# Linear attention and a softplus MLP on one core: the first tile's steps by a list, weights converted further ahead, q of the second tile on VectorE, the third batch's k maxima by GpSimd

## The chip, the cores and the metric

One core of one Trainium2 chip runs the kernel. The engines work side by side, each through its own queue in order: TensorE (PE, its weight loads PEld), VectorE (DVE), ScalarE (ACT), GpSimd (POOL) and SyncE (SP), whose queue starts nearly all transfers. The metric is device time in microseconds. Before the change three runs gave 912.88, 913.96 and 916.6 us, median 913.96.

## The reference

For each of 8 batches and 8 heads (576 tokens, 64 wide) q is turned into a softmax over its 64 channels and k into a softmax over its 576 tokens; `kv` is their sum over tokens, and the output of attention is the product of q's softmax with `kv`. All heads side by side give 4608 rows of 512 for the MLP.

```python
q_s = np.exp(q - np.max(q, axis=-1, keepdims=True))
q_s = q_s / (np.sum(q_s, axis=-1, keepdims=True) + 1e-09)
k_s = np.exp(k - np.max(k, axis=2, keepdims=True))
k_s = k_s / (np.sum(k_s, axis=2, keepdims=True) + 1e-09)
kv = np.einsum('bhsd,bhse->bhde', k_s, v)
x = np.einsum('bhsd,bhde->bhse', q_s, kv)       # then (4608, 512)
h = x @ w_in                                     # 512 to 2048
g = np.maximum(h, 0.0) + np.log1p(np.exp(-np.abs(h)))
out = g @ w_out                                  # 2048 to 512
```

## The kernel before

**Tiles and slots.** The 4608 rows are nine tiles of 512. A tile (t) has 16 slots (j), one for each 128 of the 2048 hidden columns: `up(t, j)` makes `ph` (128 hidden x 512 tokens) from x and a weight of w_in, `softplus` makes `l`, `split_g` parts it, and `down(t, j)` adds its product with w_out to the four accumulators `po`. All matmuls but the exact ones are done three times, with an operand in two parts: `hi` (rounded to the matmul's input type, ScalarE) and `lo` (the remainder, VectorE), as hi hi, lo hi, hi lo (L386 to L388 up, L418 to L420 down).

**Order.** The program is written slot by slot, and every engine takes its instructions in that order. In slot n stand `up(n)`, the slot's list of attention steps, then (before the change, tile 0 only) the weight steps, `split_g` of slot n-1, `softplus(n)`, in tile 0 the weight steps for three slots on, `down(n-2)`, and last the matmuls that the attention steps left in `waiting`. `ph` has two buffers.

**Weights.** A weight k is loaded once (L102, L103, both halves in tile `w{k}`) as 64-bit words, put together in tile 0 and kept. Per weight: `top_w` (L126) and `scale_w` (L121) on ScalarE; `sign_w`, in tile 0 on VectorE (L132), ahead of tile 0 for weights 0 to 2 on GpSimd (L134); `join_w` on VectorE (L142); and `split_w`, a cast on ScalarE (L151) and the remainder on VectorE (L152). `split_w(k)` writes into tile `w{k-1}` (weight 4 into `spare`), so it also waits until weight k-1 has been split. The first four slots of tile 0 are exact (`EXACT`): they use the joined weight itself (L381, L416) and are split only at the end of tile 0.

**Attention.** During tile t the attention of tile t+1 is made, by `PLAN`, a list of step names for each slot. `u{h}{i}` are the six steps of a k unit (a pair of heads h of one batch): 0 the maxima over a partition's tokens (L188), 1 `across` (L204), 2 subtract (L209), 3 exp and the products with v (L215, L220), 4 the reciprocal, 5 the parts of kv (L244, L247). Maxima across partitions come by two transposes on TensorE (L190, L205) while the batch number is at most `ON_PE`, and by a GpSimd reduction (L193) beyond it. `q{i}` are twelve steps of q's softmax over two halves: maxima 0, 1 (L284), 2 their swap (L271, L293), 3, 4 subtract (L296), 5, 6 exp (L299), 7, 8 totals (L302), 9 the reciprocals, 10, 11 multiply (L310); 3, 4, 10 and 11 of tile 1 go to GpSimd, of later tiles to VectorE. `x{h}{i}` transpose q (L327), take its parts (L331, L332) for the x products (L337 to L339), and part the result (L345, L346). Tile 0's own attention is made ahead of its slots from a written order; there `split_whole` (L255, L256) and `split_x0` (L373, L374) part kv and x of tile 0, in slots 0 and 1.

Of the kernel before, what the change touches and what calls it, by code (L numbers as in the profile page):

```python
# [23 lines left out]
HP = H // 2  # L24
NJ = DF // P
# [7 lines left out]

SUBS = [4] * 9

ON_PE = 2

EXACT = 4
START = [P * sum(SUBS[:t]) for t in range(len(SUBS) + 1)]
# [2 lines left out]
    "u00 u10", "u01 u11", "u02 u12", "u03 u13 q0", "u04 u14 u05 u15 q1 q2", "u20 u30 q3", "u21 u31 q4", "u22 u32",  # L42
    "u23 u33 q5 q6", "u24 u34 u25 u35 q7 q8 q9", "q10", "q11 x00 x01", "x02 x10 x11", "x12 x20 x21", "x30 x31", "",
    "x22 x32",
]
NTILE = len(SUBS)
TOK = P * max(SUBS)
# [15 lines left out]
def tile_attn_ffn(  # L63
# [9 lines left out]
    nc = tc.nc  # L73
# [65 lines left out]
    def join_w(k):  # L139

        low, high = words(k, U32)
        nc.vector.scalar_tensor_tensor(  # L142
            out=low, in0=high, scalar=3, in1=low, op0=ALU.logical_shift_left, op1=ALU.bitwise_or
        )
# [109 lines left out]
    def split_whole(h):  # L254
        nc.scalar.copy(kv_hi[0][h], whole[:, h])  # L255
        nc.vector.tensor_tensor(out=kv_lo[0][h], in0=whole[:, h], in1=kv_hi[0][h].bitcast(F32), op=ALU.subtract)  # L256
# [17 lines left out]
    def q_unit(t):  # L274

        n = TOK // 16
        half = [qtiles[t][:, 2 * g:2 * g + 2].rearrange("p h (i r) -> p (h i) r", r=32) for g in range(2)]
        m, s = (sm.tile([P, TOK // 8], F32, name=name) for name in ("m", "s"))

        def spread(a, g):  # L280
            return a[:, g * n:(g + 1) * n].unsqueeze(2).broadcast_to([P, n, 32])

        def top(g):
            nc.vector.tensor_reduce(out=m[:, g * n:(g + 1) * n], in_=half[g], op=ALU.max, axis=AX.X)  # L284

        copy = nc.vector.tensor_copy if t else nc.scalar.copy
        if t:
            slow = [nc.gpsimd if t == 1 else nc.vector] * 2
        else:
            slow = [nc.vector, nc.gpsimd]  # L290

        def join():
            nc.vector.tensor_tensor(out=m, in0=m, in1=swapped(m, copy), op=ALU.max)  # L293

        def shift(g):
            slow[g].tensor_tensor(out=half[g], in0=half[g], in1=spread(m, g), op=ALU.subtract)  # L296

        def power(g):
            nc.scalar.activation(half[g], half[g], AF.Exp)  # L299

        def total(g):
            nc.vector.tensor_reduce(out=s[:, g * n:(g + 1) * n], in_=half[g], op=ALU.add, axis=AX.X)  # L302

        def invert():
            o = swapped(s, copy)
            nc.vector.scalar_tensor_tensor(out=s, in0=s, scalar=EPS, in1=o, op0=ALU.add, op1=ALU.add)
            nc.vector.reciprocal(s, s)

        def divide(g):
            slow[g].tensor_tensor(out=half[g], in0=half[g], in1=spread(s, g), op=ALU.mult)  # L310

        return [
            lambda: top(0), lambda: top(1), join, lambda: shift(0), lambda: shift(1),
            lambda: power(0), lambda: power(1), lambda: total(0), lambda: total(1), invert, lambda: divide(0), lambda: divide(1),
        ]
# [55 lines left out]
    def split_x0(h):  # L371
        x = x_part(0, h)
        nc.scalar.copy(x[:, 0], x0[:, h])  # L373
        nc.vector.tensor_tensor(out=x[:, 1], in0=x0[:, h], in1=x[:, 0].bitcast(F32), op=ALU.subtract)  # L374
# [68 lines left out]
    with tc.manual_schedule():  # L443

        make_identity(nc, ident)
        q_load(0)
        for i in range(HP):
            place = dict(pool=xp, tag=f"x{i - 1}", shape=(P, HP * TOK)) if i >= 2 else {}
            kv_prefetch(engine=nc.vector, queue=nc.scalar, **place)
        for k in range(5):  # L450
            load_w(k)
        whole = wp.tile([P, HP, P], F32, name="spare")
        qT = wp.tile([P, HP, TOK], F32, name=f"w{NJ - 1}")
        x0 = xp.tile([P, HP, TOK], F32, name="x0")
        for z in [whole] + [z.bitcast(F32) for i in range(2) for z in kv_hi[i] + kv_lo[i]]:
            nc.vector.memset(z, 0.0)

        po = [ps_o.tile([P, DM], F32, name=f"po{h}") for h in range(HP)]  # L460
        units = [kv_unit(0, h, po[h]) for h in range(HP)]
        first = [x_first(h, po[h]) for h in range(HP)]
        todo = {f"q{i}": fn for i, fn in enumerate(q_unit(0))}
        for h in range(HP):
            todo.update({f"u{h}{i}": fn for i, fn in enumerate(units[h])})
            todo.update({f"x{h}{i}": fn for i, fn in enumerate(first[h])})
        for k in range(3):
            for name, fn in (("t", top_w), ("m", scale_w), ("s", lambda k: sign_w(k, nc.gpsimd)), ("j", join_w)):
                todo[f"{name}{k}"] = lambda k=k, fn=fn: fn(k)

        warm = ps_h.tile([P, TOK], F32, name="ph")
        todo["warm"] = lambda: [nc.tensor.matmul(warm[:, 0:P], lhsT=ident, rhs=ident, start=True, stop=True) for _ in range(8)]
        todo["kv"] = kv_prefetch
        todo["w"] = lambda: [load_w(k) for k in range(5, 10)]
        todo["q"] = lambda: [q_load(1)] + [load_w(k) for k in range(10, NJ)]
        for name in (
            "q0 q1 u00 q2 q3 q4 q5 u10 u01 u11 u02 u12 q6 u03 u13 u20 u30 u21 u31 u22 u32 t0 m0 s0 u23 u33 warm q7 q8 q9 "
            "kv kv w u04 u14 u05 u15 q10 q11 x00 x10 x01 x11 t1 m1 u24 u34 u25 u35 x20 x30 x21 x31 s1 j0 x02 x12 x22 x32 "
            "t2 m2 s2 j1 q"
        ).split():  # L480
            todo[name]()

        def attend(t):

            steps = [[] for _ in range(NJ + 1)]
            todo = {}

            def lazy(prefix, n, make):
                unit = []

                def step(i):
                    def fn():
                        if not unit:
                            unit.extend(make())
                        unit[i]()
                    return fn

                todo.update({f"{prefix}{i}": step(i) for i in range(n)})

            if t < B:  # L500
                for h in range(HP):
                    lazy(f"u{h}", 6, lambda h=h: kv_unit(t, h, banks[h % 2], after=kv_prefetch))
            lazy("q", 12, lambda: q_unit(t))
            for h in range(HP):
                lazy(f"x{h}", 3, lambda h=h: x_unit(t, h, banks[h % 2]))
            for s, names in enumerate(PLAN):
                steps[s] = [todo[name] for name in names.split() if name in todo]
            if t + 1 < NTILE:
                steps[14].append(lambda: q_load(t + 1))
            return steps  # L510

        order = [(t, j) for t in range(NTILE) for j in range(NJ)]
        pending, soft, waiting = [], None, []
        for n in range(len(order) + 3):
            slot = order[n] if n < len(order) else None
            if slot:
                t, j = slot
                if j == 0:
                    steps = attend(t + 1) if t + 1 < NTILE else [[] for _ in range(NJ + 1)]
                ph = up(t, j)  # L520
                for fn in steps[j]:
                    fn()
                if t == 0:
                    if j < 2:
                        split_whole(2 * j)
                        split_whole(2 * j + 1)
                    if j + 2 < NJ:
                        join_w(j + 2)
                        if j + 2 >= EXACT:
                            split_w(j + 2)  # L530
                    if j < 2:
                        split_x0(2 * j)
                        split_x0(2 * j + 1)
                if 0 <= n - (NJ - 2) < EXACT:
                    split_w(n - (NJ - 2))
                if j == NJ - 1:
                    for fn in steps[NJ]:
                        fn()
            if soft:
                pending.append((soft[0], soft[1] if exact(*soft[0]) else split_g(soft[1])))  # L540
                soft = None
            if slot:
                soft = slot, softplus(ph)
                if t == 0 and j + 3 < NJ:
                    for fn in (top_w, scale_w, sign_w):
                        fn(j + 3)
            while pending and order.index(pending[0][0]) <= n - 2:
                (t, j), g = pending.pop(0)
                down(t, j, g)
            for products in waiting:  # L550
                products()
            waiting.clear()
# [37 lines left out]
```

## Time and profile before

| | |
|---|---|
| profiled execution, its own time | 913.47 us |
| its span, first to last instruction | 911.7 us |
| granted TensorE clock, mean | 0.983 |
| TensorE busy | 867.4 us (95%) |
| VectorE busy | 413.3 us (45%) |
| ScalarE busy | 378.7 us (42%) |
| GpSimd busy | 50.5 us (6%) |
| DMA | 55.22 MB, 18.0% of 16 engines |

How to read it: the span is the time that the trace covers, and the rest of the execution lies around it. Busy times overlap between engines. A group of instructions is given with its line, engine, operation, tiles, form (partitions x elements) and count; in brackets stands for how long the engine sat idle before it, and whose work ended that. An "L" and a number is a line of this kernel as printed above.

### The profile page before, as it was taken

What the parts mean: (1) busy time and instruction counts of PE and PEld (TensorE: products, weight loads), DVE (VectorE), ACT (ScalarE), POOL (GpSimd) and SP (SyncE); (2) the same over time, 40 slices, a digit from 0 to 9 for tenths busy, and PEclk for the clock granted to TensorE, in tenths of its full rate; (3) what the DMA queues carried; (4) which work ended last, traced back from release to release, by engine and by line L of the source; (5) the groups of instructions that cost most, each with busy time, mean ns of one, the idle gap of its engine ahead of it and who ended that gap; (6) DMA issues with size and microseconds to landing.
All of it is one profiled execution on the core that took longest, in us unless ns stands there. A gap on an engine that the chain in (4) does not pass through costs nothing.

```text
span 911.7 us, 10863 instructions
## 1 busy us (share of the span) xinstructions
PE 867.4 (95%) x4292; PEld 701.0 (77%) x4292; DVE 413.3 (45%) x677; ACT 378.7 (42%) x596; POOL 50.5 (6%) x119
## 2 busy tenths in 40 slices
PE   3897778999999999999999999999999999999998
PEld 2455556888888888888888888888888888888886
DVE  8866676555335433544353534353435333331110
ACT  4855655625243533453345325423543334233222
POOL 2302020000001000000000000000000000000000
PEclk9899979999999999999999999999999999999999
DMA  9990101111111111110121013001300110001001
GB/s 315 379 343 0 52 0 47 47 53 52 47 47 53 52 45 48 53 53 9 57 79 49 4 47 99 25 28 47 99 1 1 46 47 1 1 1 46 1 1 46
DMA packets 49027, 55.22 MB, mean 61 GB/s; under 512 B 2256, under 2 KB 39120, under 8 KB 47824
## 3 DMA queue, kind: packets, MB, share of 16 engines
q1 hardware_dynamic: 48400, 54.27, 18.0%
q8 instruction: 33, 0.54, 0.2%
q10 hardware_dynamic: 576, 0.26, 0.1%
q14 instruction: 18, 0.15, 0.1%
HBM read 45.09 MB, written 9.44 MB: 60 GB/s over the span
## 4 chain that ended last, share of the span: by engine, by line
PE 84%; DVE 7%; ACT 5%; issue 2%; DMA 1%; POOL 0%; ACTq 0%; DVEq 0%; POOLq 0%
PE ph L386 13%; PE po L420 13%; PE po L418 13%; PE po L419 13%; PE ph L388 13%; PE ph L387 13%; PE att L220 2%; DVE w L132 2%; DVE w L142 2%; ACT w L126 1%; ACT w L121 1%; PE att L338 1%; PE att L339 1%; PE att L337 1%; DMA qt<-in_q 1%
## 5 line engine op out<-in xcount | busy, mean ns | idle before, releaser
L418 PE MATMUL po<-w,g_hi 128*128 128x512 f32 x524 | 205.9, 393 | 9.2 <-ACT g_hi L399 9.2
L420 PE MATMUL po<-w,g_lo 128*128 128x512 f32 x524 | 205.9, 393 | 3.4 <-DVE g_lo L400 3.4
L386 PE MATMUL ph<-x,w 128*128 128x512 f32 x524 | 208.0, 397 | 0.0
L419 PE MATMUL po<-w,g_hi 128*128 128x512 f32 x524 | 205.5, 392 | 0.0
L387 PE MATMUL ph<-x,w 128*128 128x512 f32 x524 | 205.2, 392 | 0.0
L388 PE MATMUL ph<-x,w 128*128 128x512 f32 x524 | 205.1, 391 | 0.0
L400 DVE TENSOR_TENSOR g_lo<-l,g_hi 128x512 fp32r<-128x512 f32 x140 | 97.5, 697 | 231.1 <-ACT g_hi L399 231.1
L394 ACT ACTIVATE l<-ph 128x512 f32<-128x512 f32 x144 | 86.2, 599 | 193.9 <-PE ph L388 193.7
L399 ACT CAST g_hi<-l 128x512 fp32r<-128x512 f32 x140 | 86.8, 620 | 120.3 <-PE po L419 117.8
L418 PEld LDWEIGHTS po<-w,g_hi 128*128 128x128 f32 x524 | 99.2, 189 | 30.6 <-ACT g_hi L399 10.3
L420 PEld LDWEIGHTS po<-w,g_lo 128*128 128x128 f32 x524 | 99.3, 189 | 26.0 <-DVE g_lo L400 5.5
L419 PEld LDWEIGHTS po<-w,g_hi 128*128 128x128 f32 x524 | 99.4, 190 | 20.9
L388 PEld LDWEIGHTS ph<-x,w 128*128 128x128 f32 x524 | 99.0, 189 | 21.3
L386 PEld LDWEIGHTS ph<-x,w 128*128 128x128 f32 x524 | 99.5, 190 | 20.3 <-issue 0.3
L387 PEld LDWEIGHTS ph<-x,w 128*128 128x128 f32 x524 | 99.2, 189 | 19.9 <-issue 0.3
L346 DVE TENSOR_TENSOR x<-att,x 128x512 fp32r<-128x512 f32 x32 | 21.4, 691 | 105.7 <-ACT x L345 105.7
L345 ACT CAST x<-att 128x512 fp32r<-128x512 f32 x32 | 18.0, 589 | 69.1 <-PE att L339 38.7
L188 DVE TENSOR_REDUCE mx<-kvt 128x128 f32<-128x640 f32 x30 | 39.3, 1318 | 11.0 <-POOL mx L193 7.6
L331 ACT CAST q_hi<-att 128x512 fp32r<-128x512 f32 x32 | 18.8, 587 | 51.3 <-DVE att L327 33.5
L332 DVE TENSOR_TENSOR q_lo<-att,q_hi 128x512 fp32r<-128x512 f32 x32 | 22.1, 692 | 32.8 <-ACT q_hi L331 32.8
L244 ACT ACTIVATE kv_hi<-att,r 64x64 fp32r<-64x64 f32 x56 | 17.4, 310 | 34.4 <-DVE r L231 30.4
L193 POOL PARTITION_ALL_REDUCE mx<-mx x20 | 14.1, 705 | 297.6 <-DVE mx L188 230.5
(108 smaller groups left out, 783.3 us busy)
## 6 DMA issues: line engine op xcount, KB each, us to landing
kvt<-in_kv SPq DMA_DIRECT2D x30, 512.0 KB, 5.3
qt<-in_q SPq DMA_DIRECT2D x9, 1024.0 KB, 4.8
out<-w SPq DMA_DIRECT2D x36, 256.0 KB, 2.1
w<-in_w_in SPq DMA_DIRECT2D x16, 512.0 KB, 10.2
w<-in_w_out SPq DMA_DIRECT2D x16, 512.0 KB, 10.2
kvt<-in_kv_tail SPq DMA_DIRECT2D x28, 64.0 KB, 4.8
x<-in_kv SPq DMA_DIRECT2D x2, 512.0 KB, 9.2
kvt<-in_kv_tail ACTq DMA_DIRECT2D x2, 64.0 KB, 6.2
```

The lines of the kernel that those rows point to most:

```text
L188: nc.vector.tensor_reduce(out=mx, in_=kt.rearrange("p c z d -> p z d c"), op=ALU.max, axis=AX.X)
L332: nc.vector.tensor_tensor(out=q_lo, in0=ps, in1=q_hi.bitcast(F32), op=ALU.subtract)
L346: nc.vector.tensor_tensor(out=x[:, 1], in0=ps, in1=x[:, 0].bitcast(F32), op=ALU.subtract)
L386: nc.tensor.matmul(ph, lhsT=w_hi, rhs=x_hi, start=h == 0, stop=False)
L387: nc.tensor.matmul(ph, lhsT=w_lo, rhs=x_hi, start=False, stop=False)
L388: nc.tensor.matmul(ph, lhsT=w_hi, rhs=x_lo, start=False, stop=h == HP - 1)
L394: nc.scalar.activation(l, ph, AF.Softplus)
L399: nc.scalar.copy(g_hi, l)
L400: nc.vector.tensor_tensor(out=g_lo, in0=l, in1=g_hi.bitcast(F32), op=ALU.subtract)
L418: nc.tensor.matmul(po, lhsT=g_hi[:, ms], rhs=w_hi, start=j == 0, stop=False)
L419: nc.tensor.matmul(po, lhsT=g_hi[:, ms], rhs=w_lo, start=False, stop=False)
L420: nc.tensor.matmul(po, lhsT=g_lo[:, ms], rhs=w_hi, start=False, stop=j == NJ - 1)
```

## The change

Three things are changed. `ON_PE` goes from 2 to 1, so the k maxima of the third batch (made during tile 1) come by GpSimd. The passes of tile 1's q that subtract and multiply go from GpSimd to VectorE. And tile 0 has a list of its own, `FIRST`, with a line for each slot: what stands ahead of the dot is issued in place of the attention and weight steps, what stands behind it after `softplus`. Its new names: `t`, `m`, `v`, `j`, `h` are `top_w`, `scale_w`, `sign_w` on VectorE, `join_w` and `split_w` of a weight, `W` and `X` `split_whole` and `split_x0` of a pair of heads, `g` is `split_g` of the slot before (for the exact slots it makes no instruction), and `Q` the load of q for tile 2. Tops, scalings and signs now run four slots ahead (before three), joins three (before two), and the split of weight j+2 stands behind `softplus(j)` (before: ahead of `split_g` and `softplus`, in the same slot).

```diff
--- before.py
+++ after.py
@@ -33,7 +33,7 @@
 
 SUBS = [4] * 9
 
-ON_PE = 2
+ON_PE = 1
 
 EXACT = 4
 START = [P * sum(SUBS[:t]) for t in range(len(SUBS) + 1)]
@@ -42,6 +42,24 @@
     "u00 u10", "u01 u11", "u02 u12", "u03 u13 q0", "u04 u14 u05 u15 q1 q2", "u20 u30 q3", "u21 u31 q4", "u22 u32",
     "u23 u33 q5 q6", "u24 u34 u25 u35 q7 q8 q9", "q10", "q11 x00 x01", "x02 x10 x11", "x12 x20 x21", "x30 x31", "",
     "x22 x32",
+]
+FIRST = [
+    "u00 u10 j2 W0 W1 W2 W3 g . t3 m3 v3 t4 m4 v4",
+    "u01 u11 X0 X1 j3 g . t5 m5 v5",
+    "u02 u12 j4 X2 X3 g . h4 t6 m6 v6",
+    "u03 u13 j5 g q0 . h5 t7 m7 v7",
+    "u04 u14 j6 u05 u15 g q1 . h6 t8 m8 v8",
+    "u20 u30 j7 g q2 j8 . h7 t9 m9 v9",
+    "u21 u31 g q3 j9 . h8 t10 m10 v10",
+    "u22 u32 g q4 j10 . h9 t11 m11 v11",
+    "u23 u33 q5 q6 g j11 . h10 t12 m12 v12",
+    "u24 u34 u25 u35 q7 q8 g j12 . h11 t13 m13 v13",
+    "g q9 q10 x00 j13 . h12 t14 m14 v14",
+    "x01 g x10 q11 j14 . h13 t15 m15 v15",
+    "x02 x11 x20 g j15 . h14",
+    "x12 x21 x30 g . h15",
+    "x31 g Q .",
+    "g .",
 ]
 NTILE = len(SUBS)
 TOK = P * max(SUBS)
@@ -285,7 +303,7 @@
 
         copy = nc.vector.tensor_copy if t else nc.scalar.copy
         if t:
-            slow = [nc.gpsimd if t == 1 else nc.vector] * 2
+            slow = [nc.vector] * 2
         else:
             slow = [nc.vector, nc.gpsimd]
 
@@ -507,43 +525,52 @@
                 steps[s] = [todo[name] for name in names.split() if name in todo]
             if t + 1 < NTILE:
                 steps[14].append(lambda: q_load(t + 1))
-            return steps
-
+            return todo, steps
+
+        CONVERT = {
+            "t": top_w, "m": scale_w, "s": lambda k: sign_w(k, nc.gpsimd), "v": sign_w, "j": join_w, "h": split_w
+        }
         order = [(t, j) for t in range(NTILE) for j in range(NJ)]
         pending, soft, waiting = [], None, []
+
+        def split_soft():
+            nonlocal soft
+            if soft:
+                pending.append((soft[0], soft[1] if exact(*soft[0]) else split_g(soft[1])))
+                soft = None
+
         for n in range(len(order) + 3):
             slot = order[n] if n < len(order) else None
+            late = []
             if slot:
                 t, j = slot
                 if j == 0:
-                    steps = attend(t + 1) if t + 1 < NTILE else [[] for _ in range(NJ + 1)]
+                    ops, steps = attend(t + 1) if t + 1 < NTILE else ({}, [[] for _ in range(NJ + 1)])
+                    if t == 0:
+                        for k in range(NJ):
+                            ops.update({f"{c}{k}": lambda fn=fn, k=k: fn(k) for c, fn in CONVERT.items()})
+                        for h in range(HP):
+                            ops.update({f"W{h}": lambda h=h: split_whole(h), f"X{h}": lambda h=h: split_x0(h)})
+                        ops.update(g=split_soft, Q=lambda: q_load(2))
                 ph = up(t, j)
-                for fn in steps[j]:
-                    fn()
                 if t == 0:
-                    if j < 2:
-                        split_whole(2 * j)
-                        split_whole(2 * j + 1)
-                    if j + 2 < NJ:
-                        join_w(j + 2)
-                        if j + 2 >= EXACT:
-                            split_w(j + 2)
-                    if j < 2:
-                        split_x0(2 * j)
-                        split_x0(2 * j + 1)
+                    before, after = FIRST[j].split(".")
+                    for name in before.split():
+                        ops[name]()
+                    late = [ops[name] for name in after.split()]
+                else:
+                    for fn in steps[j]:
+                        fn()
                 if 0 <= n - (NJ - 2) < EXACT:
                     split_w(n - (NJ - 2))
                 if j == NJ - 1:
                     for fn in steps[NJ]:
                         fn()
-            if soft:
-                pending.append((soft[0], soft[1] if exact(*soft[0]) else split_g(soft[1])))
-                soft = None
+            split_soft()
             if slot:
                 soft = slot, softplus(ph)
-                if t == 0 and j + 3 < NJ:
-                    for fn in (top_w, scale_w, sign_w):
-                        fn(j + 3)
+            for fn in late:
+                fn()
             while pending and order.index(pending[0][0]) <= n - 2:
                 (t, j), g = pending.pop(0)
                 down(t, j, g)
```

Three places in the queues, in the order of the program on the engine; `w7`, `w8` and so on are the weights' tiles, and the number behind the second underscore is a buffer's. First ScalarE in slot 6 of tile 0. Before, a cast of weight 8 (into `w7`), g of slot 5, softplus of slot 6, top and scaling of weight 9:

```order
L151 CAST w7_609<-w8_307 128x1024
L399 CAST g_hi_612<-l_579 128x512
L394 ACTIVATE l_616<-ph_590 128x512
L126 ACTIVATE w9_310<-w9_310 128x1024
L121 ACTIVATE w9_310<-w9_310 128x1024
```

Now g and softplus come first, then the cast of weight 8, then top and scaling of weight 10:

```order
L417 CAST g_hi_610<-l_579 128x512
L412 ACTIVATE l_616<-ph_593 128x512
L169 CAST w7_618<-w8_307 128x1024
L144 ACTIVATE w10_357<-w10_357 128x1024
L139 ACTIVATE w10_357<-w10_357 128x1024
```

The cast moved behind softplus and the tops a slot ahead. Second VectorE in the same slot, from the k maxima `across` (`m1`) on. Before, join and remainder of weight 8, g, and the sign of weight 9:

```order
L204 TENSOR_REDUCE m1_603<-att0_105 128x1
L204 TENSOR_REDUCE m1_605<-att1_106 128x1
L142 SCALAR_TENSOR_TENSOR w8_307<-w8_307 128x1024
L152 TENSOR_TENSOR w7_609<-w8_307,w7_609 128x1024
L400 TENSOR_TENSOR g_lo_613<-l_579,g_hi_612 128x512
L132 TENSOR_SCALAR w9_310<-w9_310 128x1024
```

Now g comes first, the subtraction from a half of q (`qt`, from GpSimd's queue), the join of weight 9, the remainder of weight 8 and the sign of weight 10:

```order
L222 TENSOR_REDUCE m1_606<-att0_105 128x1
L222 TENSOR_REDUCE m1_608<-att1_106 128x1
L418 TENSOR_TENSOR g_lo_611<-l_579,g_hi_610 128x512
L314 TENSOR_TENSOR qt_355<-qt_355,m_462 128x1024
L160 SCALAR_TENSOR_TENSOR w9_310<-w9_310 128x1024
L170 TENSOR_TENSOR w7_618<-w8_307,w7_618 128x1024
L150 TENSOR_SCALAR w10_357<-w10_357 128x1024
```

The join moved ahead by one weight, against the remainder that follows it. Third VectorE where the first x product's operand `q_lo` is made (slots 10 and 11 of tile 0). Before, from g of slot 9 on:

```order
L400 TENSOR_TENSOR g_lo_829<-l_793,g_hi_828 128x512
L132 TENSOR_SCALAR w13_366<-w13_366 128x1024
L327 STREAM_TRANSPOSE att0_105<-qt_355 128x512
L332 TENSOR_TENSOR q_lo_865<-att0_105,q_hi_864 128x512
L142 SCALAR_TENSOR_TENSOR w13_366<-w13_366 128x1024
L152 TENSOR_TENSOR w12_869<-w13_366,w12_869 128x1024
L400 TENSOR_TENSOR g_lo_873<-l_832,g_hi_872 128x512
```

Now, from g of slot 9 on, with the swap and the reciprocals of q's totals, and a multiplication of a half of q, in this stretch:

```order
L418 TENSOR_TENSOR g_lo_821<-l_787,g_hi_820 128x512
L289 COPY other_824<-s_463 32x64 x4
L324 SCALAR_TENSOR_TENSOR s_463<-s_463,other_824 128x64
L325 RECIPROCAL s_463<-s_463 128x64
L328 TENSOR_TENSOR qt_355<-qt_355,s_463 128x1024
L345 STREAM_TRANSPOSE att0_105<-qt_355 128x512
L160 SCALAR_TENSOR_TENSOR w13_366<-w13_366 128x1024
L170 TENSOR_TENSOR w11_836<-w12_363,w11_836 128x1024
L150 TENSOR_SCALAR w14_369<-w14_369 128x1024
L350 TENSOR_TENSOR q_lo_868<-att0_105,q_hi_867 128x512
```

The reciprocals of q came here from the slot before, and the multiplication from GpSimd; `q_lo` stands behind the join of weight 13, the remainder of weight 12 and the sign of weight 14, where it stood right behind the sign of weight 13 and its transpose.

## The prediction

> **What bounds the kernel now.** I read the page's 40 slices first, then the busy time by stretches, then TensorE's waits.
>
> ```profile
> PE   3897778999999999999999999999999999999998
> ```
> ```profile
> 33.60:163.20 129.60, 107.17 (x442) 73.06 (x441) 91.67 (x118) 80.34 (x105) 15.62 (x17) 0.91 0.32 116
> 163.20:911.70 748.50, 744.73 (x3741) 617.37 (x3739) 293.97 (x496) 282.31 (x462) 24.43 (x86) 1.00 0.12 39
> ```
>
> The slices (TensorE, tenths of 22.8 us each) dip only up to the seventh, about 160 us. The two stretches (length, then busy us of PE, PE loads, DVE, ACT, POOL, then granted clock) part the run where up(1,0), the first matmuls of tile 1, begin. From there to the end nothing holds TensorE: a saving there must be TensorE work. Ahead of it lie 129.6 us, tile 0, with every engine partly idle (VectorE 38 us) and a mean clock of 0.91. Who TensorE waits for in that stretch (sum, times, longest):
>
> ```profile
> PE po L418 <- ACT g_hi L399: 9.2, 2, 7.7
> PE att L190 <- DVE mx L188: 5.7, 3, 4.0
> PE po L420 <- DVE g_lo L400: 3.4, 3, 2.2
> PE att L337 <- DVE q_lo L332: 3.3, 2, 2.3
> ```
>
> With 0.8 us of L205 these are 22.4 us, all on VectorE or ScalarE. Why, a slot of VectorE's and ScalarE's timelines shows (start, duration, idle before):
>
> ```profile
> 76.63 1.21 DVE L142 SCALAR_TENSOR_TENSOR w<-w 128x1024 uint32<-128x1024 uint32 x1
> 79.08 1.23 DVE L152 TENSOR_TENSOR w<-w,w 128x1024 fp32r<-128x1024 f32 x1 [1.25 <-ACT w L151]
> 80.23 0.69 DVE L400 TENSOR_TENSOR g_lo<-l,g_hi 128x512 fp32r<-128x512 f32 x1
> 82.16 1.33 DVE L132 TENSOR_SCALAR w<-w 128x1024 uint8<-128x1024 uint8 x1 [1.24 <-ACT w L121]
> 83.52 0.49 DVE L204 TENSOR_REDUCE m<-att 128x1 f32<-128x128 f32 x2
> ```
> ```profile
> 77.93 1.13 ACT L151 CAST w<-w 128x1024 fp32r<-128x1024 f32 x1 [5.34 <-DVE w L142]
> 78.96 0.61 ACT L399 CAST g_hi<-l 128x512 fp32r<-128x512 f32 x1
> 79.48 0.59 ACT L394 ACTIVATE l<-ph 128x512 f32<-128x512 f32 x1
> 79.97 1.16 ACT L126 ACTIVATE w<-w 128x1024 uint32<-128x1024 uint8 x1
> 81.00 1.13 ACT L121 ACTIVATE w<-w 128x1024 f32<-128x1024 f32 x1
> ```
>
> ScalarE's cast of a weight (L151) waits for VectorE's join (L142), VectorE's remainder (L152) for that cast, and its sign (L132) for ScalarE's scaling (L121), all of it within one slot: VectorE idles 1.24 us twice, ScalarE 5.34 us once. The two engines take turns and TensorE waits at the end.
>
> **Prices.** Starts follow one another some 0.1 us sooner than durations say, so: sign, join, remainder 1.1 to 1.15 us each on VectorE, g_lo 0.6; on ScalarE cast, top, scaling 1.03 each, g_hi and softplus 0.5.
>
> ```profile
> L188 DVE TENSOR_REDUCE mx<-kvt 128x128 f32<-128x640 f32 x7 | 8.9, 1289 | 0.1
> L209 DVE TENSOR_TENSOR kvt<-kvt,att 128x640 f32<-128x640 f32 x4 | 3.2, 846 | 0.0
> L296 DVE TENSOR_TENSOR qt<-qt,m 128x1024 f32<-128x1024 f32 x1 | 1.2, 1224 | 0.0
> L247 DVE SCALAR_TENSOR_TENSOR kv_lo<-att,r,kv_hi 64x64 fp32r<-64x64 f32 x8 | 2.3, 283 | 1.2 <-ACT kv_hi L244 1.0
> ```
>
> So a pair of k maxima is 2.45, a pair of shifts 1.5, four kv_lo 1.15, and a pass over half of q (L296 and the reductions of the same 128x1024) 1.15 to 1.2. The transposes and remainders of 128x512 I take like L400, 0.6. TensorE:
>
> ```profile
> 46.54 3.76 PE L416 MATMUL po<-w,l 128*128 128x512 f32 x8
> 50.14 3.59 PE L381 MATMUL ph<-x,w 128*128 128x512 f32 x8
> ```
> ```profile
> 163.19 0.39 PE L386 MATMUL ph<-x,w 128*128 128x512 f32 x1
> 185.53 1.39 PE L220 MATMUL att<-kvt 128*64 128x65 f32 x40
> 279.63 1.39 PE L220 MATMUL att<-kvt 128*64 128x65 f32 x40
> 372.95 1.39 PE L220 MATMUL att<-kvt 128*64 128x65 f32 x40
> ```
>
> An exact down (L416) costs 3.6 us from start to start, an exact up (L381), 0.17 shorter by the durations, 3.43. A steady tile, products to products, is 93.3 us for 384 matmuls, of which 6.5 are attention (two products of 1.35, four x products of 0.95, below): 0.227 each, so 2.73 for an up or a down. Tile 0's TensorE work from 33.6 to up(1,0) is a steady tile (93.3) with four exact ups and downs (+6.4), without its last two downs (-5.5) and with eight transposes (+1.5): 96 us. Of 129.6 us some 33 are lost: 22.4 idle, the rest slow clock.
>
> **Part one, the list of steps.** The number of weight operations stays, and the signs of tile 0 are VectorE's already (L132). What moves: the join goes a slot earlier than the cast that needs it, tops and scalings two slots ahead of the join, the cast and remainder behind softplus. So cast h(j+2) finds join(j+2) done a slot before, and VectorE no longer idles for a cast of the same moment. What remains of waits I followed slot by slot with the prices above, each engine in its order. The new wait: sign v(j+4) stands behind scaling m(j+4), that behind h(j+2), that behind softplus(j); queued behind v on VectorE are the next slot's attention steps, g_lo and join. A cast also overwrites the tile before its own, so it waits for the remainder of the weight before; in the table that is later than its own join in slots 10 to 12 only, by at most 1.2 us of ScalarE, which has them to spare there.
>
> **Part two, q of tile 1 to VectorE.** Four GpSimd passes (two L296, two L310) become VectorE work: 4 x 1.2 = 4.8 us more. What it takes away:
>
> ```profile
> 115.34 5.55 POOL L310 TENSOR_TENSOR qt<-qt,s 128x1024 f32<-128x1024 f32 x2 [12.67 <-DVE s L307]
> 119.04 2.40 DVE L400 TENSOR_TENSOR g_lo<-l,g_hi 128x512 fp32r<-128x512 f32 x1
> ```
>
> This g_lo took 2.40 instead of 0.69 us beside GpSimd's passes, and ended 0.55 us after them. Three more VectorE instructions beside such passes were longer too, so about 3 us of the 4.8 come back. [...]
>
> **Table for tile 0.** It starts from a row of before that the change leaves alone; TensorE's up(0) starts at 33.6 in both.
>
> ```profile
> 35.56 2.55 DVE L188 TENSOR_REDUCE mx<-kvt 128x128 f32<-128x640 f32 x2
> ```
>
> VectorE's work is the sum of a slot's list, idle its waits for ScalarE. So slot 5: maxima 2.45, joins 7 and 8 2.3, g_lo 0.6, the swap of q's maxima 0.95 (five small operations, an estimate), remainder 1.15, sign 1.1. Slot 9: reciprocals 0.5, kv_lo 1.2, q's totals 2.35, g_lo 0.6, join, remainder and sign 3.4.
>
> ```
> slot  VectorE work, idle, done   up(j) done  TensorE waits
> 0     6.7   1.35   43.6          37.1        1.3 L190 (as before)
> 1     3.85  0      47.45         41.8        2.1 L205
> 2     6.1   0.75   54.3          47.75
> 3     4.55  2.95   61.8          54.8
> 4     6.4   0      68.2          62.5
> 5     8.55  0      76.75         68.85       (before: 4.0 here)
> 6     5.55  0      82.3          75.6
> 7     6.65  0      88.95         81.5
> 8     4.0   3.25   96.2          86.95       (before: 1.5 + 0.6)
> 9     8.05  0.25   104.5         93.8
> 10    7.3   0      111.8         99.25       1.4 for g_lo(8)
> 11    6.4   0      118.2         106.15      3.5 for q_lo of x0
> 12    4.75  0      122.95        117.8
> 13    3.6   0.3    126.85        124.2
> ```
>
> An up ends a down, an up, the slot's products and the waits behind the one before: up(9) at 86.95 + 2.73 + 1.35 + 2.73. How the marked cells come out. **Slot 1**: the new v3 and v4 stand ahead of `across`, which the second transposes need. Softplus(0) ends at 38.25, four more ScalarE passes at 42.45, v4 at 43.6, the maxima at 44.0; TensorE, free at 41.8, starts up(2) at 44.3 (before 43.1): the change loses 1.2 us here. **Slots 5 and 8 to 9**: VectorE now has the maxima at 70.65, before TensorE asks at 72.45, so the 4.0 us wait goes. ScalarE's pile in slot 8 is as before:
>
> ```profile
> 97.57 1.28 ACT L215 ACT_TABLE_LOAD   x1
> 98.87 1.38 ACT L215 ACTIVATE kvt<-kvt 128x640 f32<-128x640 f32 x2
> 100.15 1.99 ACT L299 ACTIVATE qt<-qt 128x1024 f32<-128x1024 f32 x2
> ```
>
> Two table loads, two exps and two q exps come to 6 us (in slot 3, without the q exps, to 4, and VectorE idles 2.95), so g_hi(7) is ready at 90.2 and VectorE idles 3.25. It then carries 8.05 us in slot 9, gets g_lo(8) out at 101.1, and TensorE, which reaches it at 99.7, waits 1.4. **Slot 11**: VectorE is 5 us behind; q_lo of x0 ends at 112.4, TensorE is free at 108.9. This 3.5 us wait takes the place of the 7.7 us one. It costs clock too:
>
> ```profile
> 140.88 0.32 PE L337 MATMUL att<-q_hi,kv_hi 128*128 128x64 f32 x1 [2.26 <-DVE q_lo L332]
> 142.71 0.63 PE L386 MATMUL ph<-x,w 128*128 128x512 f32 x1
> 143.99 0.60 PE L386 MATMUL ph<-x,w 128*128 128x512 f32 x1
> 144.90 0.40 PE L386 MATMUL ph<-x,w 128*128 128x512 f32 x1
> ```
>
> After 2.26 us idle in before, two L386 three matmuls apart start 1.28 us apart, 0.43 each instead of 0.227, and the six matmuls of an x product took 1.83 us (so 0.95 at full clock). By 144.90, where the next three have taken 0.91, 1.7 us are lost (0.88 + 0.60 + 0.23). I count that once. [...]
>
> From 124.2 the rest is TensorE's: three downs, two ups and two x products, 15.5 us: up(1,0) at **139.7**, against 163.2. The sum agrees: 33.6 + 96.3 work + 8.1 waits + 1.7 clock. Gain 23.5.
>
> What hides the rest: the loads. Top t5 now starts at 44.0; its tile must be there:
>
> ```profile
> 29.56 0.43 SPq L103 DMA_DIRECT2D w<-in_w_out  x1
> DMA to landing us min/median/max: 6.0/10.2/11.6
> ```
>
> Issued at 29.56, by the longest landing there at 41.2: covered by 2.8 us. SP's order is the same.
>
> **Part three, the third batch on GpSimd.** Eight transposes leave TensorE in tile 1. That tile took 94.1 us between its products and the next one's, the next tile, already without them, 93.3: gain **0.8**. GpSimd's reductions add a wait for VectorE, but
>
> ```profile
> 257.78 0.73 POOL L193 PARTITION_ALL_REDUCE mx<-mx  x1 [40.89 <-DVE mx L188]
> ```
>
> each is 0.73, and later tiles with them let TensorE wait nowhere. [...]
>
> **Sum.** 913.47 (profiled execution; span 911.7 and 1.8 around it; 0.5 below the median of the three runs) - 23.5 - 0.8 = 889.2.
>
> **Rivals.**
> 1. TensorE alone binds: VectorE's lag in slots 8 to 11 does not arise. Then 1.4, 3.5 and 1.7 go as well: **882.6**. For it: VectorE's durations include waits that I cannot see. Against: its 82.5 us of work in slots 0 to 13 leave little.
> 2. The waits cost more: each of the other three stalls takes a slowed window (5 us) and 0.1 us per handover, two a slot, 3 us: **897**. For it: 2.1 us of waits have slowed a window in before.
> 3. Slower: the loop closes. If VectorE stays behind by more than the 10.9 us of TensorE work between up(j) and down(j), less its own path of 7.3, that is by over 3.6 us in every slot, each slot is up 2.7, softplus to scaling 3.6, v 1.1, attention 2, g 0.6: 10 us. Before, 50.1 to 163.2, up(3) to up(1,0), are 8.7 a slot: 13 x 1.3 = 17 us more, **930**. Against: the lag is 5 us in two slots and shrinks in slots 12 and 13.
> 4. No effect: the list only swaps one turn-taking for another, 911 to 916. Against: the order puts a slot between join and cast.
>
> **How the numbers follow.** Forecast 0.60 (885 to 894), rival 1 0.14, 2 0.17, 3 0.04, 4 0.05. Faster by over 0.5% (4.6 us, about what a measurement tells from no change) 0.91, within 0.05, slower 0.04. The range takes in rivals 1 and 2: 882 to 898.
>
> **What would show it.** Right: VectorE idle in tile 0 from 38 us to about 10, no wait for L151 on L142, up(1,0) near 140, tile 1 at 93.3. Wrong: TensorE waiting over 5 us in slots 2 to 9, up(1,0) after 150, a wait in tile 1, or tops waiting for loads.

## The result, and the profile after

The changed kernel takes **893.94 us** (median of 4 runs, 893.63 to 894.55) against 915.28 (4 runs, 912.88 to 918.2) for the kernel before beside it: a ratio of **0.9766**, 95% interval 0.9734 to 0.9798. The forecast was 889.2, in a range of 882 to 898. Profile against profile it is 913.47 to 893.87 us, 19.6 less where 24.3 were forecast.

Line numbers are now those of the changed kernel: L169 and L170 are the cast and remainder of a weight, L160 the join, L150 the sign, L139 the scaling, L412 softplus, L417 and L418 g_hi and g_lo, L206 the k maxima, L222 `across`, L208 and L223 the two transposes, L314 and L328 the passes of q, L345 the transpose of q, L350 q_lo, L355 the first matmuls of an x product, L399 and L434 the exact up and down, L404 to L406 the other ups, L238 the products with v. TensorE's line of the page's 40 slices after the change:

```profile
PE   3699989999999999999999999999999999999998
```

The dip that reached the seventh slice now ends with the second, but for an 8 in the sixth. The two stretches, cut where up(0) and up(1,0) begin (length, busy us of PE, PE loads, DVE, ACT, POOL, clock):

```profile
34.00:144.50 110.50, 99.62 (x441) 69.23 (x440) 92.33 (x122) 80.82 (x105) 4.91 (x14) 0.98 0.36 134
144.50:892.00 747.50, 743.79 (x3733) 616.83 (x3731) 293.36 (x491) 282.27 (x462) 26.66 (x90) 1.00 0.12 39
```

All but one microsecond of the gain lies in tile 0: 110.5 us, where 129.6 were before and 106.1 (33.6 to 139.7) forecast. VectorE is idle there for 110.50 - 92.33 = 18.2 us (before 37.9, forecast about 10). Whom TensorE waits for in tile 0 (sum, times, longest):

```profile
PE att L355 <- DVE q_lo L350: 3.9, 1, 3.9
PE att L223 <- DVE m L222: 3.1, 2, 2.2
PE po L438 <- DVE g_lo L418: 2.2, 1, 2.2
PE att L208 <- DVE mx L206: 1.7, 2, 0.9
```

10.9 us of waits, where 22.4 were before and 8.1 stand in the forecast's sum. The 7.7 us wait for g_hi and the 4.0 us one for the maxima are gone. What slot 6 now looks like on VectorE (the stretch in which it idled 1.24 us twice before):

```profile
80.91 0.49 DVE L222 TENSOR_REDUCE m<-att 128x1 f32<-128x128 f32 x2
81.31 0.68 DVE L418 TENSOR_TENSOR g_lo<-l,g_hi 128x512 fp32r<-128x512 f32 x1
81.91 1.22 DVE L314 TENSOR_TENSOR qt<-qt,m 128x1024 f32<-128x1024 f32 x1
83.05 1.22 DVE L160 SCALAR_TENSOR_TENSOR w<-w 128x1024 uint32<-128x1024 uint32 x1
84.18 1.22 DVE L170 TENSOR_TENSOR w<-w,w 128x1024 fp32r<-128x1024 f32 x1
85.32 1.34 DVE L150 TENSOR_SCALAR w<-w 128x1024 uint8<-128x1024 uint8 x1
```

Not one has an idle time behind it in brackets: each starts when the one before it lets it. The turn-taking is gone here. But in the slots ahead of it VectorE still waits for ScalarE, and ScalarE for something else. These are ScalarE's softplus in slots 2, 3 and 5, and VectorE's remainder in slots 2 and 3 with the k maxima of slot 5:

```profile
52.20 0.60 ACT L412 ACTIVATE l<-ph 128x512 f32<-128x512 f32 x1 [4.44 <-PE po L434]
59.22 1.28 ACT L412 ACT_TABLE_LOAD   x1 [0.63 <-PE po L434]
73.41 0.60 ACT L412 ACTIVATE l<-ph 128x512 f32<-128x512 f32 x1 [1.93 <-PE po L434]
```
```profile
53.84 1.23 DVE L170 TENSOR_TENSOR spare<-w,spare 128x1024 fp32r<-128x1024 f32 x1 [1.89 <-ACT spare L169]
62.14 1.23 DVE L170 TENSOR_TENSOR w<-w,w 128x1024 fp32r<-128x1024 f32 x1 [2.72 <-ACT w L169]
72.12 2.44 DVE L206 TENSOR_REDUCE mx<-kvt 128x128 f32<-128x640 f32 x2
```

Softplus(2) waits 4.44 us, and the releaser is a matmul of down (L434), not of up. Softplus writes `l`, which has two buffers. In the four exact slots no parts are made of `l`, and down reads it itself, so softplus(2) needs the buffer that down(0) is still reading. That had not been in the forecast's table, where softplus(j) follows up(j).

One wait of a cast for its own join is left as well, in slot 5:

```profile
75.78 1.12 ACT L169 CAST w<-w 128x1024 fp32r<-128x1024 f32 x1 [1.77 <-DVE w L160]
```

`FIRST` puts the joins of weights 4 to 7 into the slots of their own splits, ahead of the dot. Only from weight 8 on does a join run a slot ahead of the cast that needs it, and three slots ahead of the matmuls.

### The profile page after: what moved, and what is told of

It reads as the page before. It is cut to its first block, busy times and chain, and to the rows that moved or that the text cites. A ratio compares the mean times of both kernels' runs of the same rounds, so it can differ in the third digit from the quotient of the medians.

```text
span 892.0 us, 10843 instructions
## 1 busy us (share of the span) xinstructions
PE 857.4 (96%) x4284; PEld 695.1 (78%) x4284; DVE 413.4 (46%) x677; ACT 379.1 (43%) x596; POOL 42.0 (5%) x119
## 4 chain that ended last, share of the span: by engine, by line
PE 87%; DVE 4%; DMA 4%; ACT 2%; issue 1%; SPq 1%; POOL 0%; ACTq 0%; DVEq 0%; POOLq 0%
PE ph L404 14%; PE po L438 14%; PE po L436 14%; PE po L437 14%; PE ph L406 14%; PE ph L405 13%; DMA w<-in_w_in 2%; PE att L238 2%; DMA w<-in_w_out 1%; PE att L356 1%; PE att L357 1%; PE att L355 1%; DVE w L150 1%; DMA qt<-in_q 1%; DVE w L160 1%
## 5 line engine op out<-in xcount | busy, mean ns | idle before, releaser
L418 DVE TENSOR_TENSOR g_lo<-l,g_hi 128x512 fp32r<-128x512 f32 x140 | 95.9, 685 | 241.1 <-ACT g_hi L417 241.0
L404 PE MATMUL ph<-x,w 128*128 128x512 f32 x524 | 206.9, 395 | 0.0
L406 PE MATMUL ph<-x,w 128*128 128x512 f32 x524 | 204.6, 390 | 0.0
L412 ACT ACTIVATE l<-ph 128x512 f32<-128x512 f32 x144 | 86.3, 600 | 204.8 <-PE ph L406 198.3
L417 ACT CAST g_hi<-l 128x512 fp32r<-128x512 f32 x140 | 86.8, 620 | 122.2 <-PE po L437 121.9
L406 PEld LDWEIGHTS ph<-x,w 128*128 128x128 f32 x524 | 98.7, 188 | 21.1
L404 PEld LDWEIGHTS ph<-x,w 128*128 128x128 f32 x524 | 99.0, 189 | 20.1 <-issue 0.3
L206 DVE TENSOR_REDUCE mx<-kvt 128x128 f32<-128x640 f32 x30 | 39.4, 1319 | 11.1 <-POOL mx L211 8.4
L350 DVE TENSOR_TENSOR q_lo<-att,q_hi 128x512 fp32r<-128x512 f32 x32 | 22.1, 691 | 31.8 <-ACT q_hi L349 31.8
L211 POOL PARTITION_ALL_REDUCE mx<-mx x24 | 16.9, 704 | 365.9 <-DVE mx L206 284.9
```

The costliest lines, as they stand in the source:

```text
L206: nc.vector.tensor_reduce(out=mx, in_=kt.rearrange("p c z d -> p z d c"), op=ALU.max, axis=AX.X)
L350: nc.vector.tensor_tensor(out=q_lo, in0=ps, in1=q_hi.bitcast(F32), op=ALU.subtract)
L404: nc.tensor.matmul(ph, lhsT=w_hi, rhs=x_hi, start=h == 0, stop=False)
L406: nc.tensor.matmul(ph, lhsT=w_hi, rhs=x_lo, start=False, stop=h == HP - 1)
L412: nc.scalar.activation(l, ph, AF.Softplus)
L417: nc.scalar.copy(g_hi, l)
```

## The experiments

Each is named by what it changes. Runs of one set share a chip and its runs of the kernel before, whose median was 913.7 us in the first set, 914.02 in the second and 913.94 in the third.

**1. A third buffer for `l`, in the changed kernel.**

```diff
-    tp = ctx.enter_context(tc.tile_pool(name="tp", bufs=2))
+    tp = ctx.enter_context(tc.tile_pool(name="tp", bufs=3))
```

> The changed kernel with three buffers for softplus's output l instead of two; nothing else. Theory A (an exact slot's softplus(j) has to wait until down(j-2) has read the same l buffer, and this, in slots 2 to 5, put VectorE some 4 us behind my table): softplus(2) starts at about 48.8 instead of 52.2, VectorE's k maxima of slot 5 at about 68.6 instead of 72.1, up(1,0) at 140 to 141 instead of 144.5, time 889 to 891. Rival B (VectorE's own work, or slow clock, makes the lag): softplus starts earlier but up(1,0) stays within 1 us of 144.5, time 893 to 895.

Measured 892.54 us (890.49 to 892.87), ratio 0.9773 [0.9756, 0.9789]; the profiled execution took 890.49. Its stretch of tile 0, and its softplus(2):

```profile
34.04:141.20 107.16, 99.38 (x441) 69.21 (x440) 92.33 (x122) 81.07 (x105) 4.93 (x14) 0.98 0.37 138
```
```profile
48.55 0.60 ACT L412 ACTIVATE l<-ph 128x512 f32<-128x512 f32 x1 [0.84 <-PE ph L399]
```

Softplus(2) starts 3.65 us sooner and waits for up (L399) alone; tile 0 is 3.3 us shorter, VectorE's idle time 14.8. VectorE's waits in slots 2 to 5, 6.7 us in the change, come to 4.3. So the place is as Theory A has it, but the time isn't: the median lies between its 891 and Rival B's 893, only the profiled execution is in Theory A's range, and the ratio is no better than the change's 0.9766, measured in another set. Both kernels again, side by side in the second set:

> The changed kernel again, on the same chip as the next three, so that they can be compared with it: 893 to 895.

> Three buffers for l again, beside the changed kernel. Theory A (the buffer is a part of what my table missed): 1.5 to 3.5 us below the changed kernel in the same runs, and up(1,0) near 141. Rival B: within 0.5 us of it.

The change took 892.28 us (891.63 to 895.73), ratio 0.9772 [0.9757, 0.9788]; with three buffers 890.66 (889.98 to 892.26), ratio 0.9745 [0.9732, 0.9758]. So the third buffer is worth about 1.6 us in the medians, with intervals that just touch. Its profiled execution this time had a tile 0 of 109.3 us (110.5 in the change's beside it) and up(1,0) at 143.0 where 141 was expected, for a reason of its own. One group of eight matmuls, up(2) behind the wait in slot 1, in the repeat:

```profile
44.15 0.52 PE L223 MATMUL att<-ident,m 128*128 128x128 f32 x2 [2.22 <-DVE m L222]
44.51 5.32 PE L399 MATMUL ph<-x,w 128*128 128x512 f32 x8
```

and in the first run:

```profile
44.53 0.52 PE L223 MATMUL att<-ident,m 128*128 128x128 f32 x2 [2.20 <-DVE m L222]
44.89 3.62 PE L399 MATMUL ph<-x,w 128*128 128x512 f32 x8
```

The same wait to 0.02 us, and 1.7 us of slow clock in one execution (granted clock 0.67 in these matmuls) and none in the other (1.00).

**2. The same buffer in the kernel before.**

> The kernel before with three buffers for l. If the buffer held the kernel before as well, it gains some 4 us (909 to 911). Theory A says it does not: there softplus(2) stood behind a cast that waited for its join anyway, so 913 to 916, within 1 us of before in the same runs.

913.72 against 913.7 us, ratio 1.0006 [0.9993, 1.002]: nothing. In the kernel before, softplus(2) stands behind a cast that waits 4.15 us for its join. The buffer becomes a limit only when the list has taken that wait away.

**3. The list alone**, with tile 1's q on GpSimd and the third batch's maxima on TensorE as before:

```diff
-ON_PE = 1
+ON_PE = 2
...
-            slow = [nc.vector] * 2
+            slow = [nc.gpsimd if t == 1 else nc.vector] * 2
```

> The list of tile 0 alone: k maxima of the third batch on TensorE and q of tile 1 on GpSimd, as before. If the list is the gain, 894 to 896.5: tile 1 gives back 1.0 us of transposes, and tile 0 moves by less than 1.5 us either way, since VectorE saves 4.8 us of passes but waits some 3 us beside GpSimd's. If the passes' contention with GpSimd was a main part of what was lost, 898 or more.

902.77 us (902.33 to 904.38), ratio 0.9887 [0.9871, 0.9902]: by the ratios some 10 us above the whole change (0.9766, 0.9772 and 0.9775 in its three sets of runs), and outside the 894 to 896.5 of the first branch; experiment 8 gives one to two of them to the third part. GpSimd's passes, and VectorE and TensorE beside them:

```profile
77.71 5.68 POOL L314 TENSOR_TENSOR qt<-qt,m 128x1024 f32<-128x1024 f32 x2 [16.21 <-DVE m L311]
116.99 3.79 POOL L328 TENSOR_TENSOR qt<-qt,s 128x1024 f32<-128x1024 f32 x2 [15.86 <-DVE s L325]
```
```profile
78.68 2.94 DVE L170 TENSOR_TENSOR w<-w,w 128x1024 fp32r<-128x1024 f32 x1
81.54 3.02 DVE L150 TENSOR_SCALAR w<-w 128x1024 uint8<-128x1024 uint8 x1
...
118.94 0.73 DVE L345 STREAM_TRANSPOSE att<-qt 128x512 f32<-128x512 f32 x1 [2.10 <-POOL qt L328]
119.58 2.29 DVE L160 SCALAR_TENSOR_TENSOR w<-w 128x1024 uint32<-128x1024 uint32 x1
```
```profile
PE att L223 <- DVE m L222: 6.5, 2, 4.3
```

A remainder takes 2.94 us (1.22 elsewhere), a sign 3.02 (1.34), a join 2.29 (1.22), and the transpose of q waits 2.10: 6.6 us, of which the first 3.4 come right ahead of the `across` that TensorE waits for. Tile 0 is 118.1 us long, 7.6 more than the change's, and about half of that is slow clock on TensorE. Behind its wait for `across`:

```profile
84.94 0.69 PE L223 MATMUL att<-ident,m 128*128 128x128 f32 x2 [4.28 <-DVE m L222]
85.27 0.78 PE L404 MATMUL ph<-x,w 128*128 128x512 f32 x1
...
90.54 0.56 PE L436 MATMUL po<-w,g_hi 128*128 128x512 f32 x1
```

The wait is 4.28 us where the change has 0.86, and the twelve up matmuls behind it take 5.27 us at a granted clock of 0.50, where the change's take 2.85 at 1.00. Ten matmuls behind the wait for g_lo(8) take 3.98 us at 0.57, against 2.42 at 1.00, though that wait is no longer here (2.0 us) than there (2.2). These three differences are 7.4 of the 7.6 us.

**4. The second part alone**, tile 1's q on VectorE in the kernel before:

```diff
-            slow = [nc.gpsimd if t == 1 else nc.vector] * 2
+            slow = [nc.vector] * 2
```

> The kernel before with q of tile 1 on VectorE alone. With the turn-taking of before every VectorE pass lengthens its slot by 1.2 us unless it fits into a wait: 4 x 1.2 more, about 3 less of blocking, so 0 to +2 us against before. If the blocking beside GpSimd held the slots, it gains 3 us or more.

919.49 us (916.68 to 921.35), ratio 1.0062 [1.0039, 1.0085]: slower by 5.7 in the medians, where 0 to 2 were expected. The five runs fall apart, 916.7 and 916.9 at a mean clock of 0.989 and 919.5 to 921.4 at 0.98, so the cost is 3 us at the least. VectorE in slot 5 of this kernel, whose line numbers are those of before:

```profile
74.89 1.21 DVE L296 TENSOR_TENSOR qt<-qt,m 128x1024 f32<-128x1024 f32 x1
76.02 1.22 DVE L142 SCALAR_TENSOR_TENSOR w<-w 128x1024 uint32<-128x1024 uint32 x1
78.49 1.23 DVE L152 TENSOR_TENSOR w<-w,w 128x1024 fp32r<-128x1024 f32 x1 [1.25 <-ACT w L151]
```

The pass stands ahead of the join, the join ahead of ScalarE's cast, the cast ahead of the remainder: it does not fill VectorE's idle 1.25 us but lengthens the chain that makes it. Tile 0 is 134.2 us long in the profile, against 129.6.

**5. `across` ahead of the sign of weight 4 in slot 1**, from experiment 1's kernel:

```diff
-    "u00 u10 j2 W0 W1 W2 W3 g . t3 m3 v3 t4 m4 v4",
-    "u01 u11 X0 X1 j3 g . t5 m5 v5",
+    "u00 u10 j2 W0 W1 W2 W3 g . t3 m3 v3 t4 m4",
+    "u01 u11 v4 X0 X1 j3 g . t5 m5 v5",
```

> Three buffers for l, and the sign of weight 4 behind the maxima of slot 1 instead of ahead of them. TensorE's 2.2 us wait in slot 1 shrinks to about 1. If VectorE's queue binds tile 0 from slot 3 on, the time stays within 0.7 us of three buffers alone, since VectorE's later steps start no sooner. If every wait of TensorE counts, it gains 1.2 us or more.

891.48 us (890.75 to 892.3), ratio 0.9752 [0.9739, 0.9765]. TensorE's waits:

```profile
PE att L355 <- DVE q_lo L350: 3.9, 1, 3.9
PE att L223 <- DVE m L222: 1.0, 2, 0.9
```

The 2.2 us wait in slot 1 is down to 0.2, and the one for q_lo is 3.9 us instead of 2.3: TensorE arrives sooner at an instruction that VectorE ends hardly sooner (q_lo starts at 114.02 us, 114.19 in experiment 1). No gain: 0.8 us above experiment 1, with intervals that overlap.

**6. The joins of weights 6 and 12 put where VectorE waits** (slots 3 and 8), with signs five ahead and the edit of experiment 5. Two more things moved with it: the join of weight 7 goes a slot ahead, and in slot 9 `g` (of slot 8) goes ahead of q's totals, `q7` and `q8`. The core of it:

```diff
-    "u03 u13 j5 g q0 . h5 t7 m7 v7",
+    "u03 u13 j5 g q0 j6 . h5 t8 m8 v8",
...
-    "u23 u33 q5 q6 g j11 . h10 t12 m12 v12",
-    "u24 u34 u25 u35 q7 q8 g j12 . h11 t13 m13 v13",
+    "u23 u33 q5 q6 g j11 j12 . h10 t13 m13 v13",
+    "u24 u34 u25 u35 g q7 q8 . h11 t14 m14 v14",
```

> As before, and tops, scalings and signs five slots ahead; the join of weight 6 moves into VectorE's wait in slot 3 and that of weight 12 into its wait in slot 8. The number of instructions stays. If VectorE's dense stretch (slots 4 to 11) binds, the first x product's q_lo comes some 2 us sooner, TensorE's wait there falls from 2.3 to under 1 us, up(1,0) at 137 to 139.5, and the time is 2 to 4 us below three buffers alone. If ScalarE binds (its two passes more in slots 1 and 2, its pile in slot 8), no gain or a loss of up to 2 us.

889.67 us (888.13 to 889.99), ratio 0.9728 [0.9715, 0.9742]: 2.6 below the change on the same chip (its interval lies clear of the change's), but only 1.0 below experiment 1, where 2 to 4 were expected and the intervals overlap. Its waits:

```profile
PE att L355 <- DVE q_lo L350: 4.1, 1, 4.1
PE att L208 <- DVE mx L206: 1.6, 2, 0.8
PE ph L405 <- DVE w L170: 0.6, 1, 0.6
PE att L223 <- DVE m L222: 0.2, 1, 0.2
```

q_lo starts 78.0 us after up(0), 2.2 sooner than in experiment 1, as expected, and the wait for g_lo(8) is gone, as its `g` no longer stands behind q's totals (2.35 us in the change). But the wait for q_lo is not under 1 us: it is longer, 4.1, since TensorE is earlier still, and up(1,0) comes at 140.6. Which of the moves brought what was not tested.

**7. That q_lo ahead of three weight steps**, from experiment 6's kernel:

```diff
-    "g q9 q10 x00 j13 . h12 t15 m15 v15",
-    "x01 g x10 q11 j14 . h13",
+    "g q9 q10 x00 . t15 m15",
+    "x01 h12 g j13 x10 q11 v15 j14 . h13",
```

> The list with three buffers of l and the joins in VectorE's waits, and now in slots 10 and 11 the first x product's q_lo ahead of the join of weight 13, the remainder of weight 12 and the sign of weight 15 (3.4 us of VectorE work, done behind it instead). Theory (VectorE's order decides when TensorE gets q_lo; VectorE has over 6 us idle from there to the end of tile 0, so what is put back costs nothing): q_lo about 2 us sooner, as ScalarE's q_hi becomes the next thing late; TensorE's wait for it 4.1 to under 2.5 us, and with less waiting less slow clock; 1.5 to 3.5 us below the version it starts from. Rival (VectorE's sum of work binds tile 0, whatever its order): the wait comes back one or two slots later, for the remainder of weight 12 or 13, and the time is the same within 0.8 us.

> The same kernel as the one with the joins in VectorE's waits, for the comparison on this chip: 888 to 891 us.

887.87 us (886.75 to 889.26), ratio 0.9713 [0.9692, 0.9735], beside 889.77 (887.29 to 891.93), ratio 0.9734 [0.9712, 0.9757], for experiment 6's kernel again. Where TensorE waits for q_lo now:

```profile
108.01 0.30 PE L355 MATMUL att<-q_hi,kv_hi 128*128 128x64 f32 x1 [1.29 <-DVE q_lo L350]
...
117.66 0.30 PE L355 MATMUL att<-q_hi,kv_hi 128*128 128x64 f32 x1 [2.56 <-DVE q_lo L350]
```

The 4.1 us wait became 1.3, and 2.6 came back at the next x product: the rival's return, though at q_lo and not at a remainder. Tile 0 is 106.4 us long (105.4 and 106.8 in the two profiles of experiment 6), and the stretch behind it 747.5 in both profiles of this set. What parts these two, 1.8 us, lies ahead of tile 0, where the edit changes nothing: tile 0 starts at 32.2 us here and at 35.0 there. The last matmuls there, in this run and then in experiment 6's again:

```profile
28.67 3.67 PE L375 MATMUL po<-w,spare 128*128 128x512 f32 x8 [3.22 <-DVE w L372]
```
```profile
28.45 6.69 PE L375 MATMUL po<-w,spare 128*128 128x512 f32 x8 [2.89 <-DVE w L372]
```

They ran at a granted clock of 1.00 in one and 0.53 in the other. The medians are 1.9 us apart and the intervals overlap: that it beats experiment 6 is not shown. That it beats the change is: the change took 893.42 us in this set, ratio 0.9775 [0.9754, 0.9796].

**8. The change without its third part** (`ON_PE = 2`), beside the change:

> The change without its third part: the k maxima of the third batch go by TensorE's transposes again. Theory (tile 1 is bound by TensorE, and eight transposes cost it 0.8 us): 0.6 to 1.2 us slower than the change, tile 0 the same length (110.5 us), tile 1 at 94.1 from products to products. Rival (the GpSimd reductions buy something else, such as an earlier attention): over 2 us slower, or no difference because other work fills the place of the transposes.

> The change itself, for the comparisons on this chip: 891 to 895 us.

895.41 us (893.75 to 897.07), ratio 0.9795 [0.9772, 0.9818], against 893.42 (892.65 to 894.16): 2.0 us in the medians, with intervals that overlap. The profiles tell it more sharply. Where tile 1 and its neighbours' products begin, without the third part:

```profile
143.46 0.39 PE L404 MATMUL ph<-x,w 128*128 128x512 f32 x1
...
259.89 1.39 PE L238 MATMUL att<-kvt 128*64 128x65 f32 x40
```

and with it:

```profile
144.12 0.39 PE L404 MATMUL ph<-x,w 128*128 128x512 f32 x1
...
259.59 1.39 PE L238 MATMUL att<-kvt 128*64 128x65 f32 x40
```

116.43 us against 115.47: the eight transposes cost 0.96 us, 0.48 of it ahead of tile 1's own products and 0.48 behind them. Tile 0, which this part leaves alone, is 111.2 us long against 110.6: behind a wait of 2.1 us in slot 1 its eight up matmuls took 5.32 us without the third part and 3.62 with it, as in experiment 1.

## Why the prediction was right, and what it mis-sized

**The bound and the place of the gain: right.** Tile 0 held what could be gained, VectorE and ScalarE taking turns was the reason, and the list nearly ends it: VectorE's idle time falls by half and the two large waits go. The prediction says that each join goes a slot ahead of its cast, and the text ahead of it that joins run three slots ahead; both hold from weight 8 on only, and the sign "no wait for L151 on L142" came out but for the 1.77 us in slot 5. From up(1,0) on, 747.5 us are left of 748.5. The list moves joins, casts, tops, scalings and signs at once, and no run parts them.

**Part one, the waits: places mostly right, sizes short.** The table had 1.3 us in slot 0, 2.1 in slot 1, none in slots 5 and 6, 1.4 for g_lo(8) and 3.5 for q_lo (8.3, where its sum has 8.1). Measured: 0.8, 2.2, two of 0.86, 2.2 and 3.9. The 1.3 counts the transposes in, from the end of up(0) to up(1), and this stretch is 1.25 now. The slow clock behind q_lo was priced at 1.7 us, and is 1.7:

```profile
117.24 0.30 PE L355 MATMUL att<-q_hi,kv_hi 128*128 128x64 f32 x1 [3.87 <-DVE q_lo L350]
...
118.61 0.63 PE L404 MATMUL ph<-x,w 128*128 128x512 f32 x1
...
121.17 0.46 PE L404 MATMUL ph<-x,w 128*128 128x512 f32 x1
```

The x product took 1.37 us instead of 0.95 (granted clock 0.74), and six up matmuls 2.56 instead of 6 x 0.227 = 1.36 (0.50); the seventh a little over its time.

**The step that was mis-sized** is the table's idle column of slots 2 to 5. It follows softplus(j) from the end of up(j) and leaves out a wait: that for one of the two buffers of `l`, which down(j-2) reads in the exact slots. Between 48 and 72 us VectorE idles 1.89 + 0.86 + 2.72 + 0.83 + 0.43 = 6.7 us, where the table has 3.7, and its k maxima end at 74.56 instead of 70.65. The lag of 4 us stays and grows a little: q_lo of x0 ends at 117.2, against 112.4 in the table. With the third buffer the same waits are 4.3 and 4.8 us in the two profiles, and q_lo ends 80.8 us after up(0) starts instead of 83.2 (78.8 in the table). That shows the mechanism, and that it is not the whole of the lag. Its worth in time is less sure: 3.3 us in one pair of profiles, 1.2 in the other, 1.6 in the medians of one chip. The medians with the third buffer, 892.54 and 890.66, are still 3.3 and 1.5 above the forecast.

Tile 0 is 4.4 us longer than forecast, and 2.8 of that are waits. The rest: 110.5 less 10.9 of waits and 1.7 of slow clock leaves 97.9 us of TensorE work, where the table took 96.3. Of these 1.6 us 0.4 are slot 0's transposes, which the table has among its waits; what makes the rest was not tested.

**Part two: wrong in its price.** It counted 4.8 us more on VectorE and 3 back. Experiment 4 shows that the passes on VectorE alone cost 5.7 us in the medians, and experiment 3, less the third part, that the list without them loses 8 to 9 (7.6 in tile 0 of the profiles). GpSimd's passes cost VectorE 6.6 us there where 3 were counted, more than the 4.8 of doing them itself; with the list TensorE waits for VectorE in that place (4.28 us), and slow clock comes on top (0.50 in the twelve matmuls behind). The 3 add up as 1.7 of the prediction's 2.40 us row and 0.4, 0.5 and 0.4 of three more instructions of before: remainders of 1.61 us at 69.94 and 117.51, a sign of 1.87 at 72.62. In experiment 3 the remainder, which reads two tiles, took 2.94 us and the sign, which reads one, 3.02: both kinds were longer beside GpSimd's passes. The expectations call this blocking and contention; that it is either, the runs don't show, only the longer durations.

**Part three: right, the size in part by luck**, 0.96 us for a forecast of 0.8. The forecast took the 0.8 from 94.1 us between two tiles' products, a stretch with only four of the eight transposes in it. Without them that stretch is 93.6 us, not 93.3; the other four lie ahead of it.

**The rivals.** TensorE alone binding (882.6) didn't come: it waits 10.9 us. The second (897) was partly so, with longer waits, but one slowed stretch in the change's profile (117.24 to 121.17 us, granted clock 0.74 and then 0.50), not four. The loop did not close, since the lag stays between 4 and 5 us. The list alone is worth some 11 us of 913.7, so "no effect" is out too. The measured 893.94 lies at the edge of the forecast's own 885 to 894: the gain came the way that was forecast, at four fifths of its size.

## What to carry to other kernels

Where two engines take turns in the same slot, an edit to either is paid in series (experiment 4: four passes of 1.2 us, 5.7 us in the medians); part them first, and ask then which buffers the earlier start runs into, those that TensorE reads directly among them (here `l`, and softplus(2)'s 4.44 us). A list of waits is not a list of savings: experiments 5 to 7 took single waits of 2.2 to 2.8 us away, and most of that came back at the next thing that VectorE was late with. Two edits can have opposite signs alone and together, so a part is priced in the kernel that has the rest.

## What was not expected of the hardware

An idle time of 2.2 us was followed by 1.7 us of slow clock in one execution and by none in another of the same kernel (5.32 and 3.62 us for the same eight matmuls). The length of the wait doesn't tell which: in the same place 2.13 us were followed by 5.32 (experiment 8) and 2.23 by 3.62 (the change). The start of tile 0 differs likewise, from 31.85 to 34.98 us among executions with this change or a variant of it, and the eight matmuls ahead of it took 3.67 to 6.69 us. A difference of 1.7 us between two profiles here says nothing about an edit until the durations of the groups are compared.
